# Decoding 64-bit weights in PSUM, taking their norms from Gram products, and ordering a whole kernel anew

## The chip, the core and the metric

The kernel runs on one core of a Trainium2 chip. The core has five engines with a queue each: TensorE (PE in the profile, its weight loads PEld) multiplies and writes PSUM, VectorE (DVE), ScalarE (ACT) and GpSimd (POOL) compute, SyncE (SP) issues all DMAs of this kernel. The metric is the device time of one execution in microseconds, the median of several runs; the profile is one further execution with its own time.

## What is computed

Windowed attention with global tokens, followed by a two-layer network on its output. Batch 8, 8 heads of 64, 512 local and 32 global tokens each. The two weight matrices arrive as 64-bit floats, everything else as 32-bit.

```python
s_g = scale * q_g @ k_all.T ;  out_g = softmax(s_g) @ v_all        # k_all: global, then local
s_ll = where(abs(i - j) <= 32, scale * q_l @ k_l.T, -1e9)
s_l = concat([scale * q_l @ k_g.T, s_ll]) ;  out_l = softmax(s_l) @ [v_g, v_l]
x = concat([out_g, out_l])            # 8 x 544 rows of 512
h = x @ w_in                          # 512 x 2048
g = where(h >= 1, h, where(h <= -1, 0, (h + 1)**2 / 4))
return (g @ w_out).astype(float32)    # 2048 x 512
```

## The kernel before

**Precision.** All large products run in float16 pairs: a number x is scaled by a power of two and split into a high half (a cast) and a low half (x minus the high half); a product of two such numbers is three float16 products. So every operand needs a scale, found from a norm, then a cast and a subtraction. Transposes go by DMA or by TensorE with an identity (`turn`, L622).

**Weights.** Each matrix is 16 tiles of 128 x 512 64-bit numbers (`w_in` by `load_win` L637 straight into its place, `w_out` by `load_wout` L687 into tiles called `twin` in the trace). `decode` (L539) makes a 32-bit float of the two 32-bit words of each number. A first instruction takes the magnitude of the high word times 2^-111 into `m`, a tile of the SBUF room (ScalarE, or GpSimd where the string `mags` has "p"); a second takes the three top bits of the low word (VectorE, or two GpSimd instructions where `shifts` has "p"); a third, on VectorE, shifts `m` left by three and joins the bits. `signed` (L568), again on VectorE, joins the sign and writes the tile. `win_decode` (L641) and `wout_decode` (L693) then multiply the upper 16 bits of the magnitudes by a matrix of ones, 4 products of 128 columns for a tile of w_in, one of 512 for a tile of w_out, summed over tiles, so that every partition holds the column sums. `w_scale` (L571) takes their maximum, once for tiles 0 to 7 and 8 to 15 of w_in, three times for w_out. `halves` (L594) splits a tile by one of the ways in `CODES` (L1449), three letters for who scales, casts and subtracts; "e" scales and subtracts in PSUM with one float32 product (two records in the trace) and one of float16, and "s" keeps the magnitude in place without `signed` and multiplies by sign and scale later.

**Attention and network.** For each batch and each block of 128 rows `att_a` (L897) makes scores of two heads, exponentials, a cast and a subtraction for the probabilities' halves, and a transpose; `att_b` multiplies by v; `att_x` divides and splits. `moe1` (L1114) makes one group of four w_in tiles for 128 rows in 48 products, `act` (L1099) the activation and its halves, `moe2` the product with w_out. The first three of 16 blocks of 256 rows go that way; later ones use a Winograd form of the same product with 7 instead of 8 block products.

**Order.** The program is recorded as named steps, cut into segments of one engine each (`segments`, L172), and put in order by a list scheduler (`schedule`, L226). It takes the segment with the earliest due time on each engine, from costs (`cost`, L130) and `deadlines` (L331), counts free places in three shared stores (`ROOMS`: 48 SBUF tiles of 2 KB, 6 of 4 KB and 8 PSUM banks; `CAPS` limits each kind), and `LATER` (L1451) shifts each step's due time by a given number of microseconds. Strings in `T` (L1563) choose an engine for each small operation: `subs`, `casts`, `adds` for the probabilities of batches 0 and 1, `glow` for the low half of an activation, `lows` for that of an attention output, `splits`, `turns`, `halves`, `mags`, `shifts`. All engines execute their queue in that order. All instructions pass through one helper, so the profile puts nearly all of them on L1440; loads are on L1442.

Of the kernel before, what the change touches and what calls it, by code (L numbers as in the profile page):

```python
# [128 lines left out]

def cost(engine, op, a, k, outs, ins, tiles):  # L130
# [8 lines left out]
    if engine == "sync":  # L139
        b = o.shape[0] * n * mybir.dt.size(o.dtype)  # L140
        if op == "dma_start_transpose":
            return 1300.0, b / 186.0
        run = min(tuple(x.ap[-1])[1] * mybir.dt.size(x.dtype) for x in (o, ins[0]))
        return 560.0, b / (215.0 if run < 512 else 340.0)
    if engine == "scalar":
        ptr = any(free(x) == 1 for x in ins[1:])
        if "accum_out" in k:
            own = 190 if ptr else 95
        elif mybir.dt.size(o.dtype) == 2:
            own = 185 if ptr else 90  # L150
# [207 lines left out]
def attention_moe(nc, memory, q_l, k_l, v_l, q_g, k_g, v_g, w_in, w_out, out):  # L358
# [3 lines left out]
    P = 128  # L362
# [60 lines left out]
    ps_h = bank("ps_h")  # L423
    ps_o = bank("ps_o")
# [114 lines left out]
    def decode(words, mag, who, whom):  # L539

        raw = words.rearrange("p (c t) -> p c t", t=2)
        lo, hi = raw[:, :, 0], raw[:, :, 1]
        m = tmp.tile([P, DM], F32, tag="tmp", name="wmag")

        if whom == "p":
            nc.gpsimd.tensor_scalar(m, hi.bitcast(F32), 2.0 ** -111, 1.0, op0=ALU.mult, op1=ALU.mult)  # L550
# [14 lines left out]
    def upper(mag):  # L565
        return mag.bitcast(BF16).rearrange("p (c t) -> p c t", t=2)[:, :, 1]
# [20 lines left out]
    def scaled_id(n, s, whos):  # L587
        if not any(x[0] == "e" for x in whos):
            return None
# [4 lines left out]
    def halves(w, a, s, sid, who):  # L594
# [3 lines left out]
        if who[0] == "e":  # L598
            o = ps_h.tile([P, DM], F32, tag="p", name="wps")
# [22 lines left out]
    def turn(who, o, i):  # L622
# [5 lines left out]
        t = ps_h.tile([P, 8, P], F16, tag="p", name="turn")  # L628
# [12 lines left out]
    def win_decode(f):  # L641
        words = w32[f].bitcast(I32)
        raw = words.rearrange("p (c t) -> p c t", t=2)
        if halves_of([f])[0][0] == "s":

            decode(words, raw[:, :, 0].bitcast(F32), T["shifts"][f], T["mags"][f])
            mag = w32[f].bitcast(BF16).rearrange("p (c t) -> p c t", t=4)[:, :, 1]
        else:
            m = decode(words, None, T["shifts"][f], T["mags"][f])
            mag = upper(m)  # L650
            signed(raw[:, :, 1], raw[:, :, 1], m)
# [41 lines left out]
    def wout_decode(f):  # L693
        raw = W.pop(("rawo", f))
        m = decode(raw.rearrange("p c t -> p (c t)"), None, T["shifts"][NF + f], T["mags"][NF + f])
        mag = upper(m)
        signed(wo32[f], raw[:, :, 1], m)
        n, gs = next((n, gs) for n, gs in enumerate(WOUT) if f // WG in gs)
        f0, f1 = gs[0] * WG, (gs[-1] + 1) * WG
        if f == f0:  # L700
            W["no"] = ps_o.tile([P, DM], F32, tag="p", name=f"won{f}")
        nc.tensor.matmul(W["no"], ones, mag, start=(f == f0), stop=(f == f1 - 1))
# [3 lines left out]
        nc.vector.tensor_reduce(mx, W["no"], axis=AX.X, op=ALU.max)  # L706
# [156 lines left out]
    def moe_scales(key, d, tv, first, c0=0, c1=4):  # L863
# [8 lines left out]
        nc.vector.tensor_scalar(bd, (wt if first else W["tma"])[:, c0:c1], tv[:, 0:1], 2.0 ** 28, op0=ALU.mult, op1=ALU.mult)  # L872
# [537 lines left out]
    for name, (t, _, fn, a) in sorted(steps.items(), key=lambda x: x[1][:2]):  # L1410
# [8 lines left out]
            ps_h=4, ps_o=3, ps_s=2, ps_x=1)  # L1419
# [5 lines left out]
def build(tc, *args):  # L1425
# [4 lines left out]
    with ExitStack() as ctx:  # L1430
# [5 lines left out]
        with tc.manual_schedule():  # L1436
# [14 lines left out]
LATER = {"Lk00": -99.8, "Lk01": 23.8, "Lk02": 37.7, "Lk10": 212.4, "Lk11": -53.4, "Lk12": 178.5, "Lk20": 42.4, "Lk21": 24.7,  # L1451
# [146 lines left out]
```

## Time and profile before

| what | us |
|---|---|
| median of 3 runs | 946.48 |
| lowest and highest run | 943.96, 948.40 |
| the profiled execution | 945.8 |
| its span, first to last instruction | 944.0 |
| PE busy in the span | 861.5 |
| VectorE, ScalarE, GpSimd busy | 786.0, 642.9, 434.0 |

A busy share is an average over stages: PE is nearly idle while the first weights and keys arrive, and nearly full from 240 us on. Busy times of PE are those of its pipelined products, so what counts is when it idles. A wait names the last thing that the waiting instruction lacked, an engine with the tile that it wrote ("DVE room": a tile of the SBUF room), or a DMA.

### The profile page before, as it was taken

Reading aid. Unit: us, or ns where it says so; the run is one execution under the profiler, and the core shown is the slowest. Engines: PE = TensorE matmul, PEld = TensorE weight load, DVE = VectorE, ACT = ScalarE, POOL = GpSimd, SP = SyncE. Lnnn points to the kernel's source line nnn. Section 1 sums busy time; section 2 is a strip of 40 time slices with the busy share of each in tenths; the row PEclk is TensorE's granted clock in tenths of the full one; section 3 lists DMA queues with packets and bytes.
Section 4 is the critical chain, followed back from the end, with each engine's and each line's share of the span. In section 5 each row is a group of like instructions: output and inputs, shape, how many; then the busy total and the mean of one; then the engine's idle time right before and its main releaser. Section 6 shows DMA issues by size and latency. Waiting matters only on the chain.

```text
span 944.0 us, 30674 instructions
## 1 busy us (share of the span) xinstructions
PE 861.5 (91%) x12204; PEld 642.3 (68%) x12207; DVE 786.0 (83%) x2079; ACT 642.9 (68%) x1545; POOL 434.0 (46%) x450
## 2 busy tenths in 40 slices
PE   0466889998989998999999999999999999999998
PEld 0343757567858686667677767867686777786864
DVE  2989899889777997789989979999999897878642
ACT  3799979567767784768676757777776765565441
POOL 9154576624233634363364333554446245536231
PEclk9979999999999999999999999999999999999999
DMA  9999748958977899849995847989997777353101
GB/s 267 265 201 236 166 105 152 174 128 119 161 172 151 136 188 169 169 83 159 193 180 94 158 98 138 173 137 170 155 166 138 152 112 141 57 105 66 35 2 45
DMA packets 407823, 134.91 MB, mean 143 GB/s; under 512 B 384128, under 2 KB 393344, under 8 KB 407680
## 3 DMA queue, kind: packets, MB, share of 16 engines
q1 hardware_dynamic: 407680, 132.96, 74.6%
q8 instruction: 95, 1.56, 0.7%
q14 instruction: 48, 0.39, 0.1%
HBM read 43.52 MB, written 8.91 MB: 56 GB/s over the span
## 4 chain that ended last, share of the span: by engine, by line
PE 63%; DVE 9%; DMA 7%; ACT 3%; issue 2%; SPq 2%; POOL 1%; DVEq 0%; ACTq 0%; POOLq 0%
PE bank L1440 63%; DVE room L1440 5%; DMA room<-const_pb 3%; ACT room L1440 2%; DMA room<-room 2%; DVE bank L1440 1%; DMA room<-in_k_g_dram 1%; DMA room<-in_k_l_dram 1%; SPq L1440 1%; DMA room<-in_q_l_dram 1%; ACT junk_junk L1440 1%; DVE const_pb L1440 1%; SPq L1442 1%; POOL const_pb L1440 1%; POOL room L1440 1%
## 5 line engine op out<-in xcount | busy, mean ns | idle before, releaser
L1440 PEld LDWEIGHTS <-room 128*128 128x128 f16 (+2 forms) x5136 | 288.2, 98 | 223.5 <-issue 25.0
L1440 PE MATMUL bank<-weights_w,room 128*128 128x512 f16 x1632 | 373.1, 380 | 3.6 <-ACT room L1440 2.1
L1440 POOL TENSOR_TENSOR room<-room,room 128x512 f16<-128x512 f32 (+5 forms) x200 | 223.7, 1125 | 212.3 <-ACT room L1440 185.0
L1440 PE MATMUL bank<-room,weights_w 128*128 128x128 f16 (+1 forms) x4032 | 235.2, 216 | 6.7 <-DVE room L1440 4.0
L1440 PEld LDWEIGHTS <-weights_w 128*128 128x128 f16 x4032 | 221.1, 98 | 18.3 <-issue 5.3
L1440 POOL TENSOR_TENSOR const_pb<-room,const_pb 128x384 f16<-128x384 f32 (+1 forms) x117 | 124.2, 1063 | 225.5 <-DVE const_pb L1440 81.4
L1440 ACT CAST room<-room 128x512 f16<-128x512 f32 (+3 forms) x212 | 122.0, 583 | 81.3 <-DVE room L1440 65.3
L1440 ACT ACTIVATE room<-room,small_nb 128x192 f32<-128x192 f32 (+1 forms) x256 | 117.2, 459 | 55.2 <-DVE small_nb L1440 45.0
L1440 PE MATMUL bank<-room,room 96*128 96x64 f16 (+3 forms) x2816 | 128.3, 196 | 9.4 <-DMA room<-const_pb 6.1
L1440 PE MATMUL bank<-room,twin 128*128 128x128 f16 (+1 forms) x2160 | 123.1, 216 | 3.3 <-DMA room<-room 2.4
L1440 PEld LDWEIGHTS <-twin 128*128 128x128 f16 x2160 | 115.5, 98 | 6.3 <-DMA room<-room 2.5
L1440 DVE CUSTOM_DVE_ANT_0 room<-bank,const_mask,batch_small_q 128x192 f32<-128x192 f32 (+1 forms) x256 | 99.0, 426 | 11.2 <-PE bank L1440 10.4
L1440 ACT ACTIVATE junk_junk<-room 128x512 f16<-128x512 f32 (+1 forms) x120 | 75.2, 626 | 46.0 <-DMA room<-in_k_l_dram 16.7
L1440 ACT ACTIVATE room<-bank,batch_small_ms 128x512 f32<-128x512 f32 (+1 forms) x114 | 84.4, 750 | 28.8 <-DVE bank L1440 18.3
L1440 DVE SCALAR_TENSOR_TENSOR bank<-bank,batch_small_ms,room 128x512 f32<-128x512 f32 (+1 forms) x114 | 82.1, 724 | 16.6 <-ACT room L1440 16.5
L1440 DVE SCALAR_TENSOR_TENSOR room<-room,batch_small_ms,bank 128x512 f32<-128x512 f32 (+1 forms) x114 | 80.7, 711 | 0.8
L1440 ACT COPY room<-bank 128x512 f32<-128x512 f32 (+2 forms) x98 | 56.5, 587 | 22.3 <-PE bank L1440 20.9
L1440 DVE CAST const_pb<-room 128x384 f16<-128x384 f32 (+1 forms) x109 | 51.4, 474 | 19.9 <-DMA room<-const_pb 13.2
L1440 DVE TENSOR_TENSOR bank<-bank,room 128x512 f32<-128x512 f32 (+1 forms) x60 | 39.0, 656 | 27.0 <-PE bank L1440 26.9
L1440 DVE SCALAR_TENSOR_TENSOR room<-room,batch_small_ms,room 128x512 f32<-128x512 f32 (+1 forms) x60 | 54.1, 901 | 0.8 <-ACT room L1440 0.2
L1440 DVE TENSOR_TENSOR room<-room,room 128x512 f16<-128x512 f32 (+1 forms) x55 | 40.9, 751 | 12.7 <-ACT room L1440 12.6
L1440 ACT ACTIVATION_READ_ACCUMULATOR room<-room,small_nb 128x1 f32 x256 | 48.1, 188 | 0.0
(153 smaller groups left out, 959.1 us busy)
## 6 DMA issues: line engine op xcount, KB each, us to landing
room<-room SPq DMA_DIRECT2D x80, 128.0 KB, 3.2
weights_w<-in_moe_w_in_dram SPq DMA_DIRECT2D x32, 256.0 KB, 4.2
room<-in_q_l_dram SPq DMA_DIRECT2D x32, 256.0 KB, 4.2
twin<-in_moe_w_out_dram SPq DMA_DIRECT2D x32, 256.0 KB, 3.9
out_dram<-room SPq DMA_DIRECT2D x32, 256.0 KB, 2.7
room<-in_k_l_dram SPq DMA_DIRECT2D x24, 256.0 KB, 4.3
room<-in_v_l_dram SPq DMA_DIRECT2D x24, 256.0 KB, 3.9
room<-const_pb SPq DMA_TRANSPOSE x124, 3.4
```

The costliest lines, as they stand in the source:

```text
L1440: getattr(getattr(tc.nc, engine), op)(*a, **k)
L1442: r = tc.nc.sync.dma_start(*a)
```

## The change

The magnitudes that come from ScalarE, and all results of the third instruction that are not kept in place, lie in a PSUM bank (`ps_m`) instead of the SBUF room, so `signed` reads one operand from PSUM. [...] The float32 way of `halves` and the transposes on TensorE get bank kinds of their own. The costs of the planner change, and the order and the strings were searched anew; no DMA is added or removed but for one transpose.

```diff
 def cost(engine, op, a, k, outs, ins, tiles):
-        run = min(tuple(x.ap[-1])[1] * mybir.dt.size(x.dtype) for x in (o, ins[0]))
+        run = min(stretch(x) for x in (o, ins[0]))
         return 560.0, b / (215.0 if run < 512 else 340.0)
...
-            own = 185 if ptr else 90
+            own = 185 if ptr else 45 if ins[0].tensor.name in tiles and tiles[ins[0].tensor.name][2] else 90
...
+    if engine == "gpsimd" and o.dtype == I32:
+        return 125 + n * 3.6, 0
     if engine == "gpsimd":
         return (125 + n * (1.93 if len([x for x in ins if free(x) > 1]) > 1 else 1.05) if op != "memset" else 60 + n * 0.82), 0
...
-    if n > 16 and o.dtype == I32 and len(big) == 1:
-        return 525, 0
     if len(big) > 1 or ps or op == "tensor_reduce":
-        return (80 if op == "tensor_tensor" else 135) + m / 0.96 + (40 if "accum_out" in k else 0), 0
+        return 70 + 60 * len([x for x in ins if free(x) == 1]) + m / 0.96 + (8 if "accum_out" in k else 0), 0
...
     def decode(words, mag, who, whom):
-        m = tmp.tile([P, DM], F32, tag="tmp", name="wmag")
+        up = words.bitcast(U16).rearrange("p (c t) -> p c t", t=4)[:, :, 1]
+        m = ps_m.tile([P, DM], F32, tag="p", name="mag") if whom == "a" or mag is None else None
+        got = m
         if whom == "p":
-            nc.gpsimd.tensor_scalar(m, hi.bitcast(F32), 2.0 ** -111, 1.0, op0=ALU.mult, op1=ALU.mult)
+            got = tmp.tile([P, DM], F32, tag="tmp", name="wmag")
+            nc.gpsimd.tensor_scalar(got, hi.bitcast(F32), 2.0 ** -111, 1.0, op0=ALU.mult, op1=ALU.mult)
         else:
-            nc.scalar.activation(m, hi.bitcast(F32), AF.Abs, scale=2.0 ** -111)
+            nc.scalar.activation(got, hi.bitcast(F32), AF.Abs, scale=2.0 ** -111)
-        if who == "p":
+        if who == "a":
+            nc.scalar.activation(lo, up, AF.Copy, scale=2.0 ** -13, bias=2.0 ** -14 - 0.5)
+        elif who == "p":
...
-        nc.vector.scalar_tensor_tensor(mag.bitcast(I32), m.bitcast(I32), 3, lo, op0=ALU.logical_shift_left, op1=ALU.bitwise_or)
+        nc.vector.scalar_tensor_tensor(mag.bitcast(I32), got.bitcast(I32), 3, lo, op0=ALU.logical_shift_left, op1=ALU.bitwise_or)
...
-    def w_scale(norms, tag, n, pl, room=1.0):
+    def w_scale(squares, tag, n, pl, room=1.0):
         e, t2, t8, s = cols(pl, tag, tag, n, n, n, n)
+        root(e, squares)
+        norms = t2
+        all_max(norms, e, tag)
         nc.vector.tensor_scalar(e.bitcast(I32), norms.bitcast(I32), 0x7F000000, None, op0=ALU.bitwise_and)
-        inverse(t2, s, e, 2.0 ** -51, 2.0 ** -13 * room)
+        inverse(t2, s, e, 2.0 ** -51, 2.0 ** -10 * room)
...
     def win_decode(f):
         for k in range(NK):
-            nc.tensor.matmul(W["n"][:, f % WG], ones, mag[:, k * P:(k + 1) * P], start=(k == 0), stop=(k == NK - 1))
+            x = half[:, k * P:(k + 1) * P]
+            nc.tensor.matmul(W["n"][:, f % WG], x, x, start=(k == 0), stop=(k == NK - 1))
...
     def wout_decode(f):
-        nc.tensor.matmul(W["no"], ones, mag, start=(f == f0), stop=(f == f1 - 1))
+        for k in range(NK):
+            x = half[:, k * P:(k + 1) * P]
+            nc.tensor.matmul(W["no"][:, k], x, x, start=f == f0 and k == 0, stop=f == f1 - 1, skip_group_check=True)
...
-            ps_h=4, ps_o=3, ps_s=2, ps_x=1)
+            ps_m=3, ps_w=3, ps_t=3, ps_h=4, ps_o=3, ps_s=2, ps_x=1)
...
-T = dict(... adds="vvvvvv1vvvvvvvvvvvvvavvvvvvvvv1v",
-         subs="pppppppppppvvvpppppppvpvvpppppvp", glow="pppppppppppvpppv",
-         turns="aaaaaaaaaadddddddddddddddddddddddddddddddddddddddddddddddddd", casts="aaaaaaaaaaaaaaaavvavvvavvvvvvavv",
-         mags="aaapaaaaaaaaaaaaaaaaaaaaaaaaaaaa", lows="ppppvpvv", halves="aaaaaaaaabacacacdecchccbddfdcbef",
-         shifts="pppvpvvpvvvvvvvvvvvvvvvvvpvvvvvv", splits="vvvvvvvvvvvpvvvpvvvpvppp", ...
+T = dict(... adds="vvvvvv1vv11vvaa11vaa1vv1av1vv1v1",
+         subs="ppppppppppppppppvvpvvpvpvvppvpvv", glow="ppvppvpvvpvpppvv",
+         turns="aaaaaaaaaadddddddddddddddddddddddddddadddddddddddddddddddddd", casts="aaaaaaaaaavaavaavvavvavvvvavvaav",
+         mags="pappaaaaaaaaaaaaaaapaaaapaaaaaaa", lows="vppvvpvp", halves="aaaaaaaaaiacacacdeccdcedcifdcdef",
+         shifts="vppapvvpvpvvvvvvvvvvvvvvapavvvvv", splits="vvvvvvvvvvvpvvppvvvpppvp", ...
```
`stretch` is new and gives the longest contiguous run of bytes of an access pattern. Nearly all entries of `LATER` differ; those of the new list are fewer and mostly smaller.

More of the change, by code (lines that the diff above doesn't have):

```diff
@@ L127, in free, with stretch @@
     return n
+def stretch(ap):
+    n = 1
+    for st, c in reversed([tuple(d) for d in ap.ap][1:]):
+        if st != n and c > 1:
+            break
+        n *= c
+    return n * mybir.dt.size(ap.dtype)
 def cost(engine, op, a, k, outs, ins, tiles):
@@ L423, in attention_moe @@
     ps_h = bank("ps_h")
+    ps_m = bank("ps_m")
+    ps_w = bank("ps_w")
+    ps_t = bank("ps_t")
     ps_o = bank("ps_o")
@@ L587, in scaled_id @@
     def scaled_id(n, s, whos):
-        if not any(x[0] == "e" for x in whos):
-            return None
         t = cp.tile([P, P], F32, tag="sid", name=f"sid{n}")
@@ L598, in halves @@
         if who[0] == "e":
-            o = ps_h.tile([P, DM], F32, tag="p", name="wps")
+            o = ps_w.tile([P, DM], F32, tag="p", name="wps")
             nc.tensor.matmul(o, sid, a, start=True, stop=False)
@@ L627, in turn @@
         n = i.shape[0]
-        t = ps_h.tile([P, 8, P], F16, tag="p", name="turn")
+        t = ps_t.tile([P, 8, P], F16, tag="p", name="turn")
         for c in range(8):
@@ L643, in win_decode @@
         raw = words.rearrange("p (c t) -> p c t", t=2)
+        half = w32[f].bitcast(BF16).rearrange("p (c t) -> p c t", t=4)
         if halves_of([f])[0][0] == "s":
             decode(words, raw[:, :, 0].bitcast(F32), T["shifts"][f], T["mags"][f])
-            mag = w32[f].bitcast(BF16).rearrange("p (c t) -> p c t", t=4)[:, :, 1]
+            half = half[:, :, 1]
         else:
-            m = decode(words, None, T["shifts"][f], T["mags"][f])
-            mag = upper(m)
-            signed(raw[:, :, 1], raw[:, :, 1], m)
+            signed(raw[:, :, 1], raw[:, :, 1], decode(words, None, T["shifts"][f], T["mags"][f]))
+            half = half[:, :, 3]
         if f % WG == 0:
@@ L694, in wout_decode @@
         raw = W.pop(("rawo", f))
-        m = decode(raw.rearrange("p c t -> p (c t)"), None, T["shifts"][NF + f], T["mags"][NF + f])
-        mag = upper(m)
-        signed(wo32[f], raw[:, :, 1], m)
+        signed(wo32[f], raw[:, :, 1], decode(raw.rearrange("p c t -> p (c t)"), None, T["shifts"][NF + f], T["mags"][NF + f]))
+        half = wo32[f].bitcast(BF16).rearrange("p (c t) -> p c t", t=2)[:, :, 1]
         n, gs = next((n, gs) for n, gs in enumerate(WOUT) if f // WG in gs)
@@ L700, in wout_decode @@
         if f == f0:
-            W["no"] = ps_o.tile([P, DM], F32, tag="p", name=f"won{f}")
-        nc.tensor.matmul(W["no"], ones, mag, start=(f == f0), stop=(f == f1 - 1))
+            W["no"] = ps_o.tile([P, NK, P], F32, tag="p", name=f"won{f}")
+        for k in range(NK):
+            x = half[:, k * P:(k + 1) * P]
+            nc.tensor.matmul(W["no"][:, k], x, x, start=f == f0 and k == 0, stop=f == f1 - 1, skip_group_check=True)
         if f < f1 - 1:
@@ L705, in wout_decode @@
         mx = sm.tile([P, 1], F32, tag="womx", name=f"womx{f}")
-        nc.vector.tensor_reduce(mx, W["no"], axis=AX.X, op=ALU.max)
+        nc.vector.tensor_reduce(mx, W["no"], axis=AX.XY, op=ALU.max)
         t8, so = w_scale(mx, f"wo{n}", 1, cp)
@@ L870, in moe_scales @@
         bd, rb, s2, sg, hs, a1, a2 = [t[:, c0:c1] for t in d["ms"][:7]]
-        nc.vector.tensor_scalar(bd, (wt if first else W["tma"])[:, c0:c1], tv[:, 0:1], 2.0 ** 28, op0=ALU.mult, op1=ALU.mult)
+        nc.vector.tensor_scalar(bd, (wt if first else W["tma"])[:, c0:c1], tv[:, 0:1], 2.0 ** 26, op0=ALU.mult, op1=ALU.mult)
         nc.vector.tensor_scalar(bd, bd, 1.0, 2.0 ** 60, op0=ALU.max, op1=ALU.min)
@@ L1449 @@
 CODES = {"a": "eaa", "b": "sap", "c": "pap", "d": "aap", "e": "aav", "f": "pav", "g": "sav", "h": "eav", "i": "vap", "j": "eva"}
-LATER = {"Lk00": -99.8, "Lk01": 23.8, "Lk02": 37.7, "Lk10": 212.4, "Lk11": -53.4, "Lk12": 178.5, "Lk20": 42.4, "Lk21": 24.7,
[111 rows of a table removed]
-T = dict(late=1, fast=3, cb=200, cbs=5, lk0=4.19, lq0=1.76, lv0=30, sk=12, sq=14, adds="vvvvvv1vvvvvvvvvvvvvavvvvvvvvv1v",
-         subs="pppppppppppvvvpppppppvpvvpppppvp", glow="pppppppppppvpppv",
-         turns="aaaaaaaaaadddddddddddddddddddddddddddddddddddddddddddddddddd", casts="aaaaaaaaaaaaaaaavvavvvavvvvvvavv",
-         mags="aaapaaaaaaaaaaaaaaaaaaaaaaaaaaaa", lows="ppppvpvv", halves="aaaaaaaaabacacacdecchccbddfdcbef",
-         shifts="pppvpvvpvvvvvvvvvvvvvvvvvpvvvvvv", splits="vvvvvvvvvvvpvvvpvvvpvppp", att=1.35, s0=60, s1=100, s2=254.09,
-         wd0=4, wds=2.06, wd8=19.2, wdt=1.9, wh=1.5, whs=1.4, od=58.2, ods=2.2, oh=0.7, ohs=0.92, e0=25.78, e1=70, e2=120.0,
-         e3=156.0, w0=24.7, w1=24.34, w2=25.15, w3=25.51, z1=18.29, lq1=24, lv2=24.36, sv=34, sqb=35.02, pk2=20.4, pk3=30,
+LATER = {"Lk00": 2.5, "Lk01": -54.4, "Lk02": -50, "Lk10": 49.4, "Lk11": 1.2, "Lk12": 173.6, "Lk20": 64.2, "Lk21": 200.3,
[105 rows of a table added]
+T = dict(late=1, fast=3, cb=200, cbs=5, lk0=4.19, lq0=1.76, lv0=30, sk=12, sq=14, adds="vvvvvv1vv11vvaa11vaa1vv1av1vv1v1",
+         subs="ppppppppppppppppvvpvvpvpvvppvpvv", glow="ppvppvpvvpvpppvv",
+         turns="aaaaaaaaaadddddddddddddddddddddddddddadddddddddddddddddddddd", casts="aaaaaaaaaavaavaavvavvavvvvavvaav",
+         mags="pappaaaaaaaaaaaaaaapaaaapaaaaaaa", lows="vppvvpvp", halves="aaaaaaaaaiacacacdeccdcedcifdcdef",
+         shifts="vppapvvpvpvvvvvvvvvvvvvvapavvvvv", splits="vvvvvvvvvvvpvvppvvvpppvp", att=1.35, s0=60, s1=100, s2=254.09,
+         wd0=4, wds=2.06, wd8=19.2, wdt=1.9, wh=1.5, whs=1.4, od=58.2, ods=2.2, oh=0.7, ohs=0.92, e0=25.78, e1=70, e2=120,
+         e3=156, w0=24.7, w1=24.34, w2=25.15, w3=25.51, z1=18.29, lq1=24, lv2=24.36, sv=34, sqb=35.02, pk2=20.4, pk3=30,
          pk4=45.8, pq2=28.03, pq4=44, pv=35.24, pvs=0.33, lw=0.54, lo=32.46, los=2.12)
```

3 lines of the change are left out of this document (removed), and 216 rows, old and new, of the table LATER.

## The prediction

> **What bounds the kernel now.** I read the page first, then busy time by stretches, then who waits for whom before the first MoE product, then the groups of instructions with their shapes.
>
> ```profile
> span 944.0 us, 30674 instructions
> PE 861.5 (91%) x12204; PEld 642.3 (68%) x12207; DVE 786.0 (83%) x2079; ACT 642.9 (68%) x1545; POOL 434.0 (46%) x450
> ```
> ```profile
> core 0: us, PE busy (x) PEld busy (x) DVE busy (x) ACT busy (x) POOL busy (x), PEclk, DMA share, GB/s
> 0.00:24.00 24.00, 1.38 (x11) 1.15 (x12) 5.82 (x9) 7.14 (x13) 21.27 (x39) 1.00 0.92 266
> 24.00:94.00 70.00, 40.29 (x399) 26.98 (x400) 63.93 (x184) 62.42 (x138) 27.11 (x25) 0.93 1.01 233
> 94.00:240.00 146.00, 132.51 (x1962) 102.20 (x1960) 133.44 (x374) 113.04 (x280) 78.51 (x76) 1.00 0.73 140
> 240.00:400.00 160.00, 149.64 (x2118) 113.72 (x2116) 131.22 (x358) 110.17 (x277) 65.02 (x68) 1.00 0.91 165
> 400.00:900.00 500.00, 497.38 (x7277) 375.19 (x7274) 436.66 (x1131) 339.04 (x815) 234.18 (x233) 1.00 0.73 128
> 900.00:944.00 44.00, 40.29 (x460) 23.06 (x456) 14.92 (x29) 11.14 (x25) 7.85 (x11) 1.00 0.08 25
> ```
> Subtract PE's busy time from each stretch: PE is idle 22.6, 29.7, 13.5, 10.4, 2.6 and 3.7 us. From 400 us on TensorE is the bound and nothing but less TensorE work helps. The 66 us of idle PE before 240 us are what can be won, and there VectorE is nearly full: 63.9 of 70 us, then 133.4 of 146. In the first 24 us everybody waits for the loads (DMA share 0.92), which the change leaves as they are.
>
> ```profile
> PE bank L1440 <- DVE room L1440: 33.7, 10, 12.0
> ...
> DVE room L1440 <- DMA weights_w<-in_moe_w_in_dram: 12.8, 2, 10.2
> PE bank L1440 <- ACT weights_w L1440: 11.7, 8, 2.9
> ...
> DVE room L1440 <- POOL weights_w L1440: 4.5, 2, 2.6
> ```
> ```profile
> 94.19 2.84 PE L1440 MATMUL bank<-room,weights_w 128*128 128x128 f16 x48
> ```
> The first fence has waits before 94 us, the second the first group of MoE products. PE waits 33.7 us for VectorE and 11.7 us for ScalarE's first halves of the weights; VectorE waits 4.5 us for GpSimd's shifts. So a microsecond less on the chain loads, decode, scale, attention, first product is worth up to a microsecond of the end; one in the steady part is worth nothing.
>
> **The change, part by part.**
>
> *Magnitudes in PSUM.* Each of 32 weight tiles has two VectorE passes over 128x512 words, and both read two SBUF tiles now.
>
> ```profile
> L1440 DVE SCALAR_TENSOR_TENSOR weights_w<-weights_w,room 128x512 int32<-128x512 int32 x15 | 11.5, 777 | 0.1
> L1440 DVE SCALAR_TENSOR_TENSOR room<-room,weights_w 128x512 int32<-128x512 int32 x15 | 10.7, 717 | 17.4 <-DMA weights_w<-in_moe_w_in_dram 12.8 <-POOL weights_w L1440 4.5
> L1440 DVE SCALAR_TENSOR_TENSOR weights_w<-twin,room 128x512 int32<-128x512 int32 x7 | 6.6, 950 | 0.0
> L1440 DVE SCALAR_TENSOR_TENSOR room<-room,twin 128x512 int32<-128x512 int32 x7 | 5.4, 774 | 0.0
> ```
> ```profile
> L1440 DVE SCALAR_TENSOR_TENSOR weights_w<-twin,room x10: 676/682/1047, 94.0 to 155.6; 128x512 int32<-128x512 int32 x10
> L1440 DVE SCALAR_TENSOR_TENSOR room<-room,twin x9: 675/693/1631, 96.9 to 151.9; 128x512 int32<-128x512 int32 x9
> ```
> ```profile
> L1440 DVE SCALAR_TENSOR_TENSOR room<-room,twin 128x512 int32<-128x512 int32 x16 | 13.8, 869 | 3.2 <-ACT room L1440 1.9 <-POOL twin L1440 1.2
> L1440 DVE SCALAR_TENSOR_TENSOR weights_w<-twin,room 128x512 int32<-128x512 int32 x16 | 13.7, 854 | 0.0
> ```
> The first fence is before 94 us, the second gives min/median/max after it, the third the whole run. The median is some 685 ns and single ones take up to 1631: they stood behind something, and GpSimd's SBUF work ran beside them. With one operand in PSUM I expect the plain 685. Before 94 us that is 15 x 92 + 15 x 32 + 7 x 265 + 7 x 89 ns = 4.4 us; in the whole run 15 x 92 + 15 x 32 + 16 x 184 + 16 x 169 ns = 7.5 us. If the cause is another, it is 0.
>
> ```profile
> L1440 DVE TENSOR_TENSOR bank<-bank,room 128x512 f32<-128x512 f32 x52 | 35.6, 692 | 18.0 <-PE bank L1440 17.8 <-ACT room L1440 0.2
> L1440 DVE TENSOR_TENSOR room<-bank,small_rc 128x512 f32<-128x512 f32 x32 | 21.8, 681 | 0.8 <-PE bank L1440 0.8
> L1440 ACT ACTIVATE room<-twin 128x512 f32<-128x512 f32 x16 | 10.6, 670 | 0.0
> ```
> No row has an int32 pass on PSUM; the nearest two-operand passes on a bank take 681 and 692 ns, so I add nothing for PSUM itself (bounds: -5 to +10 ns each). [...] ScalarE's magnitude pass (670 ns into SBUF) I leave at its price; one that writes PSUM from SBUF is not in the trace, and bank-sourced copies are no slower than SBUF ones, so within 0.1 us each.
>
> *Norms by Gram products.*
> ```profile
> L1440 PE MATMUL bank<-room,const_ones 128*128 128x128 bf16 x60 | 7.3, 277 | 31.3 <-DVE room L1440 31.3
> L1440 PE MATMUL bank<-weights_w,const_sid 128*128 128x512 f32 x26 | 16.0, 698 | 0.0
> L1440 PE MATMUL bank<-weights_w,const_negid 128*128 128x512 f16 x13 | 5.1, 395 | 10.9 <-ACT weights_w L1440 10.9
> L1440 PE MATMUL bank<-room,const_ones 128*128 128x512 bf16 x13 | 5.0, 388 | 3.9 <-DVE room L1440 3.9
> ```
> w_in keeps 64 products of 128 columns; each loads its own stationary tile now, beside the product before. w_out gets 64 of 7.3/60 = 0.12 us for 16 of 0.38: +1.6 us. One tile fewer takes the float32 way through PSUM (13 to 12): (16.0 + 5.1)/13 = -1.6 us. TensorE comes out even.
>
> ```profile
> L1440 DVE TENSOR_SCALAR small_dg<-const_negid,small_amv 128x128 bf16<-128x128 f16 x8 | 2.7, 341 | 0.0
> L1440 DVE TENSOR_REDUCE small_amv<-bank 128x1 f32<-128x128 f32 x8 | 2.2, 278 | 0.4 <-PE bank L1440 0.4
> L1440 DVE TENSOR_SCALAR small_nb<-small_nb 128x2 f32<-128x2 f32 x125 | 29.6, 241 | 0.2
> ```
> Each of five scales gains a root and a maximum over the partitions: 341 + 278 + two small operations of at most 241 = 1.1 us of VectorE with one product between. Two lie before 94 us (2.2 us, on the chain to the halves), three behind (3.3 us). The norm products now read the signed words, one VectorE pass later; the next tile's passes are queued there anyway, so nothing is charged.
>
> *Codes: who does what.* The strings give ScalarE three shifts and one query turn (whose eight transposes go to TensorE, beside its idle time), and GpSimd four magnitudes for nine subtractions less; both have room after 24 us. VectorE matters:
>
> ```profile
> L1440 DVE TENSOR_TENSOR room<-room,room 128x512 f16<-128x512 f32 x42 | 31.9, 768 | 11.5 <-ACT room L1440 11.4
> L1440 DVE TENSOR_TENSOR const_pb<-room,const_pb 128x448 f16<-128x448 f32 x4 | 2.5, 621 | 0.0
> L1440 DVE TENSOR_SCALAR weights_w<-weights_w 128x512 int32<-128x512 int32 x11 | 4.9, 465 | 0.0
> L1440 POOL TENSOR_TENSOR room<-room,room 128x512 f16<-128x512 f32 x137 | 173.7, 1275 | 176.5 <-ACT room L1440 155.8 <-PE bank L1440 12.0 <-DMA room<-const_pb 3.7
> ```
> Before 94 us: one shift less, a second pass for the tile that loses its code "s": about 0, so with the scales +2.0 and the relief -4.4 the chain gains 2.4 us. After it: five MoE low halves and one attention output 6 x 768, three more subtractions of probabilities 3 x 621, the scales 3.3, eight more small additions 8 x 241, one weight tile's scaling 0.5 (another tile's low half comes, a cast goes), less two shifts and a split (1.7): 4.6 + 1.9 + 3.3 + 1.9 + 0.5 - 1.7 = 10.5 us, less 3.1 us of relief: +7.4 us of VectorE work where it idles 12.6 us. GpSimd needs 1275 ns for what VectorE does in 768, so those results come earlier. Between 0 and +7.4, I take +1.5, near the end that fits the idle time.
>
> *Costs and order.* The loads' order on SP's queue, the transposes' and every engine's order change, and no DMA is added. What the old order did not know is visible:
> ```profile
> L1440 POOL TENSOR_SCALAR weights_w<-weights_w 128x512 int32<-128x512 f32 x5 | 10.5, 2098 | 0.4
> L1440 POOL TENSOR_SCALAR weights_w<-weights_w 128x512 f32<-128x512 uint16 x5 | 5.9, 1183 | 6.1 <-DMA weights_w<-in_moe_w_in_dram 5.8
> ```
> A GpSimd shift takes 2.1 + 1.2 = 3.3 us; `cost` (L130) gave both instructions 663 ns, 1.3 us together, and now gives 663 and 1968. Five of the six belong to w_in, whose tiles all products wait for. VectorE's waits for them (4.5 us here, 1.2 us for a w_out tile) are such plan errors. PE's 11.7 us behind ScalarE come from the same queues. An order made from true prices can win from 0 to 5.7 + 11.7 = 17.4 us; I take the 5.7 and a third of the 11.7 (a row of eight waits, each under 2.9, not all removable): -9.6.
>
> **Sum** against the profiled execution (945.8 us: span 944.0 and 1.8 around it): -2.4 + 1.5 - 9.6 = -10.5, so 935.3; the median of the runs, 946.48, lies 0.7 above, so 936.0.
>
> **Rivals.**
> *No change* (943 to 950). The relief is eaten by the work moved to VectorE, and the new order is as far from the chip as the old one: -2.4 + 1.5 = -0.9, 945.6. For it: VectorE's work grows by 5 us in all, and an order made from better estimates is still one of estimates. Against: the waits above are visible and priced.
>
> *Slower: banks.* Now ScalarE's decode needs one of the eight PSUM banks that the products use.
> ```profile
> 78.75 0.65 ACT L1440 ACTIVATE room<-twin 128x512 f32<-128x512 f32 x1
> ```
> ```profile
> 81.67 0.64 DVE L1440 SCALAR_TENSOR_TENSOR weights_w<-twin,room 128x512 int32<-128x512 int32 x1
> ```
> A magnitude lives from 78.75 to 82.31, 3.6 us; the tile view above has nine or ten w_out decodes behind 94 us, beside the first products. With three magnitudes, four products' banks and one output bank all eight are gone, and the next score or product waits; on ScalarE's queue exponentials and relus stand behind a magnitude that waits. From about that filling on, nine decodes that each hold one group of 48 (2.84 us) back by half cost 12.8 us: 946.5 - 0.9 + 12.8 = 958. Against: the planner counts banks and can place w_out's decodes where scores do not need them.
>
> *More* (921). All 17.4 us of order, and half of the 10.4 us idle at 240 to 400: 946.5 - 2.4 - 17.4 - 5.2 = 921.5. For it: those later waits are order too; against: loads at full DMA share before 94 us set a floor.
>
> **How the numbers follow.** Forecast case 0.48 (926.7 to 941.6: order between -17.4 and -4, the moved work 0 or 1.5), more 0.14 (912 to 926), no change 0.20, banks 0.18 (951 to 965). A measurement of this kernel tells about 0.5% (4.7 us) from no change; faster by more is 0.48 + 0.14 = 0.62, within 0.20, slower 0.18. The range 918 to 955 leaves out half of the case of more and somewhat over half of the bank case, under 0.2 in all. The predicted time is the likeliest case's, 936.
>
> **What would show it.** Relief: the int32 passes with a bank at 680 to 700 ns mean, whatever GpSimd does. Order: the first group of 48 products before 94 us, PE's wait for ScalarE's weights well under 11.7 us, PE idle before 240 us some 55 us for 66. Scales: five more products with ones, 1 to 2 us each between the last norm and the first half. Wrong: bank tiles as releasers of ScalarE's magnitudes or of PE (the bank rival); int32 passes still at 800; the first product no earlier than 94 us; PE busy from 400 us on below 497 of 500.

## The result: 1.1 % slower, and the profile after

| | before | changed |
|---|---|---|
| median of 4 runs, us | 947.25 (943.96 to 948.40) | 957.76 (954.79 to 959.21) |
| profiled execution, its span | 945.8, 944.0 | 958.5, 956.8 |
| mean granted TensorE clock in it | 0.993 | 0.982 |

The ratio is 1.0113, with a 95% interval of 1.0076 to 1.0149. Forecast were 936 us and a range of 918 to 955.

The head of the page after, then busy time by stretches (columns: busy us and instructions of each engine, PE's clock, DMA share, GB/s):

```profile
span 956.8 us, 30761 instructions
PE 876.8 (92%) x12265; PEld 651.5 (68%) x12265; DVE 783.5 (82%) x2113; ACT 641.0 (67%) x1549; POOL 421.0 (44%) x445
```
```profile
0.00:24.00 24.00, 2.40 (x17) 1.67 (x17) 7.88 (x19) 10.07 (x23) 18.65 (x40) 1.00 0.99 259
24.00:94.00 70.00, 48.11 (x382) 30.47 (x383) 61.88 (x197) 59.55 (x130) 24.98 (x25) 0.85 1.00 232
94.00:240.00 146.00, 131.16 (x1980) 102.06 (x1978) 135.16 (x375) 111.05 (x278) 66.31 (x68) 1.00 0.71 140
240.00:400.00 160.00, 153.74 (x2148) 115.91 (x2146) 134.93 (x375) 115.47 (x290) 68.61 (x70) 0.97 0.95 164
400.00:900.00 500.00, 488.41 (x7027) 365.68 (x7024) 411.44 (x1090) 322.50 (x789) 225.86 (x222) 1.00 0.75 129
```

The row that changed sides is the steady part. From 400 to 900 us PE was idle for 2.6 us before and is idle for 11.6 us now. Followed along the same products in both traces (roughly, since their order differs), the changed kernel is some 2 us behind at 400 us, 4 at 600, 9.5 at 730 and 12.7 at 850. The loss arises where no weight is decoded any more. What PE waits for there (engine and tile waited for: us in total, times, longest):

```profile
PE bank L1449 <- DMA room<-const_pb: 6.1, 7, 1.5
PE bank L1449 <- DMA room<-room: 2.0, 2, 1.2
PE bank L1449 <- DVE room L1449: 1.2, 1, 1.2
PE bank L1449 <- DVE small_nb L1449: 0.9, 2, 0.7
PE bank L1449 <- ACT room L1449: 0.9, 2, 0.5
```

`room<-const_pb` is the transposing DMA that turns the probabilities for the product with v. Before, there was one such wait of 2.1 us. The chain of work that ended last can be followed back only to 707 us in the changed kernel. From there to 860 us, by share, in the kernel before and then in the changed one:

```profile
by line: PE bank L1440 100.1%
```
```profile
by line: PE bank L1449 44.2%; DMA room<-const_pb 10.7%; DVE room L1449 9.6%; issue 6.1%; SPq L1449 3.6%; DMA room<-in_v_l_dram 3.5%; DMA room<-in_q_l_dram 3.4%; POOL room L1449 3.0%; POOL const_pb L1449 2.8%; DMA room<-room 2.2%; DVE bank L
```

TensorE was the whole chain there and is less than half of it now. The rest is many small pieces, DMAs and SyncE's queue (SPq) among them. That queue, in the changed kernel's timeline (start, us until the last of the row is issued, count):

```profile
249.99 0.53 SPq L1451 DMA_DIRECT2D room<-in_q_l_dram  x1
250.57 0.57 SPq L1451 DMA_DIRECT2D room<-in_v_l_dram  x1
...
260.16 4.01 SPq L1449 DMA_TRANSPOSE room<-room  x3
264.27 0.53 SPq L1451 DMA_DIRECT2D room<-in_k_l_dram  x1
264.89 3.21 SPq L1449 DMA_TRANSPOSE room<-room  x2
268.20 2.00 SPq L1449 DMA_DIRECT2D room<-room  x3
...
273.92 1.83 SPq L1449 DMA_DIRECT2D room<-room  x3
275.86 1.75 SPq L1451 DMA_DIRECT2D room<-in_v_l_dram  x3
...
284.99 3.47 SPq L1449 DMA_TRANSPOSE room<-const_pb  x2
288.56 0.53 SPq L1451 DMA_DIRECT2D room<-in_q_l_dram  x1
289.19 1.18 SPq L1449 DMA_DIRECT2D qg_qgb<-qg_qga  x2
```

Between the first and the last of these rows the queue has hardly a gap: 41 issues, 13 of them transposes, take 40.4 us. The planner (`cost`, sync branch) prices a transpose at 1300 ns and another DMA at 560, which is 13 x 1.30 + 28 x 0.56 = 32.6 us. Part of the excess can be waiting: the profile puts 10.8 us of SyncE's waits for other engines into these 40.4 us, within the issues' own durations. Neither price was touched by the change; the order was sought anew under them.

PE waits 3.2 us, from 286.5 us on, for the first of the two transposes of `const_pb` at 284.99, near the end of that row. The last write into a tile of that name before it was GpSimd's:

```profile
280.10 0.92 POOL L1449 TENSOR_TENSOR const_pb<-room,const_pb 128x384 f16<-128x384 f32 x1 [0.29 <-DVE const_pb L1449]
```

It ended at 281.02 us, so that transpose was issued at least 4.0 us after its input was there, behind another transpose and three plain DMAs. Of PE's seven waits for such transposes from 400 us on, five follow one that was issued 0.7 to 4.3 us after the last such write, longer than PE then waited; in the other two (1.1 and 0.6 us) it was 0.1 and 0.4 us, and the queue does not explain them.

The planner's own end, by its own prices, is 933.5 us for the kernel before and 918.6 for the changed one: it promised 15 us that the chip did not give.

### The profile page after: what moved, and what is told of

The parts are those of the page before. It is cut to its first block, busy times and chain, and to the rows that moved or that the text cites. A ratio compares the mean times of both kernels' runs of the same rounds, so it can differ in the third digit from the quotient of the medians.

```text
span 956.8 us, 30761 instructions
## 1 busy us (share of the span) xinstructions
PE 876.8 (92%) x12265; PEld 651.5 (68%) x12265; DVE 783.5 (82%) x2113; ACT 641.0 (67%) x1549; POOL 421.0 (44%) x445
## 5 line engine op out<-in xcount | busy, mean ns | idle before, releaser
L1449 PEld LDWEIGHTS <-room 128*128 128x128 f16 (+1 forms) x5144 | 291.6, 99 | 229.9 <-issue 22.6
L1449 POOL TENSOR_TENSOR room<-room,room 128x512 f16<-128x512 f32 (+3 forms) x194 | 215.7, 1118 | 236.0 <-ACT room L1449 192.0
L1449 PEld LDWEIGHTS <-weights_w 128*128 128x128 f16 (+1 forms) x4160 | 232.1, 99 | 43.1 <-DVE weights_w L1449 24.9
L1449 POOL TENSOR_TENSOR const_pb<-room,const_pb 128x448 f16<-128x448 f32 (+1 forms) x114 | 122.5, 1075 | 191.6 <-DVE const_pb L1449 92.5
L1449 ACT CAST room<-room 128x512 f16<-128x512 f32 (+2 forms) x213 | 122.1, 582 | 87.2 <-DVE room L1449 60.8
L1449 ACT ACTIVATE room<-room,small_nb 128x224 f32<-128x224 f32 (+1 forms) x256 | 117.2, 459 | 56.6 <-DVE small_nb L1449 45.4
L1449 PE MATMUL bank<-room,room 96*128 96x64 f16 (+3 forms) x2816 | 131.6, 197 | 24.4 <-DMA room<-const_pb 13.0
L1449 DVE CUSTOM_DVE_ANT_0 room<-bank,const_mask,batch_small_q 128x224 f32<-128x224 f32 (+1 forms) x256 | 98.5, 425 | 6.1 <-PE bank L1449 3.4
L1449 DVE CAST const_pb<-room 128x448 f16<-128x448 f32 (+1 forms) x109 | 51.2, 470 | 24.9 <-DMA room<-const_pb 20.4
L1449 DVE TENSOR_TENSOR room<-room,room 128x512 f16<-128x512 f32 (+1 forms) x62 | 47.7, 774 | 12.7 <-ACT room L1449 12.5
```

Source lines behind the costliest of these rows:

```text
L1449: getattr(getattr(tc.nc, engine), op)(*a, **k)
```

## The experiments

Three theories went in. A: the new order has no room for what SyncE's queue really takes. B: the new decode costs the time. C, the prediction's own premise: from 400 us on TensorE is full whatever the order. Later ones are named in the expectations. To hold an order, each segment's due time is set to its start in the plan to be copied, and "every engine held to it" means that an engine may only take the next one:

```diff
 def plan(steps, tiles, prio, names, hop, slack, landing, ahead):
     segs = segments(steps, tiles, prio, names)
...
+    seen = {}
+    for g in segs:
+        i = seen[g.step] = seen.get(g.step, -1) + 1
+        g.prio = HELD[g.step][i]
     order, taken, _ = schedule(segs, tiles, hop, slack, landing, ahead)
...
-                    if g.ready > now:
+                    if g.ready > now or g.n != turns[e][-1]:
                         continue
```

The kernel before had a median of 946.8 to 947.8 us beside the experiments, and all ratios are to it; the changed kernel was not run again beside them.

| run | what | us | ratio, 95% interval | planner's own end |
|---|---|---|---|---|
| e1 | changed, late order as before | 944.65 | 0.9970 (0.9946 to 0.9994) | 921.2 |
| e2 | new decode, old codes, old order from 170 us | 957.85 | 1.0123 (1.0098 to 1.0149) | 934.6 |
| e3 | before, 40 issues more | 958.67 | 1.0130 (1.0097 to 1.0163) | 940.5 |
| e4 | changed, no searched shifts | 961.08 | 1.0143 (1.0115 to 1.0171) | 935.6 |
| e5 | changed, order sought with new DMA prices | 944.52 | 0.9976 (0.9958 to 0.9994) | 917.6 |
| e6 | old decode, likewise | 934.72 | 0.9887 (0.9853 to 0.9922) | 922.5 |
| e7 | changed, 30 issues fewer | 947.93 | 1.0006 (0.9990 to 1.0021) | 919.5 |
| e8 | new decode, old codes, in e6's order | 944.58 | 0.9973 (0.9957 to 0.9989) | 923.7 |
| e9 | as e5, from another start | 944.53 | 0.9969 (0.9954 to 0.9984) | 918.6 |
| e10 | as e6, other random moves | 941.70 | 0.9954 (0.9934 to 0.9974) | 920.0 |
| e11 | e8 without the longer scale chain | 939.91 | 0.9940 (0.9920 to 0.9960) | 921.5 |
| e12 | e8 with magnitudes in SBUF | 952.16 | 1.0064 (1.0045 to 1.0083) | 928.2 |

**e1, only the late order undone.**

> The changed program; up to about 430 us every engine keeps the changed kernel's order, from there on each of the five runs its segments in the order of the kernel before. Nothing is left out. Theory A (SyncE's queue): the new order puts transposing DMAs behind others in SyncE's queue just before their products are due, and from 400 us on the chain passes through that queue. With the old late order the PE waits after 430 us (about 9 us in the changed kernel) go, and the time falls by 8 to 12 us to 946-950. Theory B (the decode: banks, Gram products, ScalarE's magnitudes): the loss comes with the decode, which is untouched: 955-960. Theory C (the prediction's: from 400 us on TensorE is full whatever the order, so the loss lies before): 955-960 too, with PE's idle time after 430 us unchanged.

Measured 944.65 us, 13.1 less than the changed kernel: theory A, a little more than it expected, while B and C expected nothing. PE after 430 us, in the changed kernel and in e1 (rows of busy time, then e1's only wait):

```profile
430.00:900.00 470.00, 458.41 (x6637) 343.71 (x6636) 383.54 (x1023) 302.16 (x746) 208.65 (x206) 1.00 0.76 131
```
```profile
430.00:900.00 470.00, 466.39 (x6859) 352.64 (x6857) 403.96 (x1061) 316.77 (x766) 212.84 (x215) 1.00 0.73 131
```
```profile
PE bank L1455 <- DMA room<-const_pb: 3.6, 2, 2.4
```

The same instructions in another order give 8 us of PE back; the waits fall from 11.1 us to 3.6. The chain from 707 to 860 us is TensorE's again:

```profile
by line: PE bank L1455 100.0%
```

So the late order is the loss, and everything else of the change together is worth 944.65 - 947.84 = -3.2 us. (e1's profiled execution, at 949.78 us, is the slowest of its ten.)

**e3 and e7, the suspected cost added and taken away.** e3 cuts the swap of a query tile's halves in four. e7 replaces it by one copy and so leaves the swap out: the scores of those batches come from unswapped halves.

```diff
 def swap_q(b, c):
-        dma(u[0:D], t[D:2 * D])
-        dma(u[D:2 * D], t[0:D])
+        for h0, h1 in [(0, H // 2), (H // 2, H)] if b >= 4 else [(0, H)]:
+            dma(u[0:D, h0:h1], t[D:2 * D, h0:h1])
+            dma(u[D:2 * D, h0:h1], t[0:D, h0:h1])
```
```diff
 def swap_q(b, c):
+        if b >= 2:
+            dma(u, t)
+        else:
             dma(u[0:D], t[D:2 * D])
             dma(u[D:2 * D], t[0:D])
```

> The kernel before in its own order, every engine held to it, but in batches 4 to 7 each of the two DMAs that swap a query tile's halves is cut in two by heads: 40 more issues on SyncE, the same bytes. Theory A: an issue takes about 0.64 us of SyncE's in-order queue (three in a row 1.83 to 2.00 us in the changed kernel's trace), so 26 us of queue are added between some 390 and 820 us, where the transposes stand behind them; where SyncE is already late they end on TensorE: slower by 8 to 18 us, 955-965, with PE waits for const_pb transposes that the kernel before does not have. Theory C: TensorE is full there and SyncE waits for others half of the time, so at most 2 us: 946-949.

> The changed kernel in its own order, every engine held to it, but in batches 2 to 7 one DMA copies a query tile whole in place of two that swap its halves: 30 issues fewer on SyncE, the same bytes; the scores of those batches are left computed from unswapped halves. Theory A: 30 x 0.64 = 19 us of SyncE's queue are taken out between some 200 and 820 us, of which the part that lies ahead of late transposes comes back: faster than the changed kernel by 4 to 11 us, 947-954, with fewer PE waits for const_pb transposes. Theory B and C: as the changed kernel, 956-959.

Both as A expected. 40 issues more cost the kernel before 958.67 - 947.84 = 10.8 us, 30 fewer give the changed one 957.76 - 947.93 = 9.8 us, with the same bytes and every engine's order held. That is 0.27 and 0.33 us of the end for an issue of some 0.64 us. The planner saw the first in part (940.5 for 933.5) and the second not at all (919.5 for 918.6): in the changed kernel's order the queue costs the chip what the plan does not know. PE's waits from 400 to 900 us, the largest row of e3 and then of e7 (whose profiled execution, at 943.32 us, is the fastest of its ten):

```profile
PE bank L1448 <- DMA room<-const_pb: 8.4, 4, 3.5
```
```profile
PE bank L1458 <- DMA room<-const_pb: 2.9, 2, 1.7
```

In the kernel before PE was idle for only 2.6 us there and SyncE's issues filled some 307 of the 500 us, and still two fifths of each added issue reached the end. So the queue can be late in a burst (in the timeline above the transpose of 284.99 us was issued at least 4.0 us after its input was there, behind another transpose and three plain DMAs) while it is far from full on average. Theory C falls.

**e4, the search taken away.**

> The changed program with LATER empty: the planner's deadlines alone under the new prices, no searched shifts. The planner's own end is 935.6 us for it and 918.6 us for the changed kernel, so it holds the search to be worth 17.0 us. Theory A: what the search won it won partly in time that SyncE does not have, so on the chip it is worth well under 17 us: 957 plus 3 to 12, so 960-969. Theory B and C: prices right enough, the search is worth what it says: about 974.

Measured 961.08, in A's range. By the planner the searched shifts are worth 17.0 us; on the chip 961.08 - 957.76 = 3.3, which the two intervals do not tell from nothing.

**e5 and e6, the order sought with new DMA prices.** Both issue prices go up, and `LANDING`, the planner's time from the end of a transfer to its use, goes down:

```diff
         if op == "dma_start_transpose":
-            return 1300.0, b / 186.0
+            return 1500.0, b / 186.0
-        return 560.0, b / (215.0 if run < 512 else 340.0)
+        return 680.0, b / (215.0 if run < 512 else 340.0)
...
-HOP, SLACK, LANDING, AHEAD = 290.0, 600.0, 1500.0, 5
+HOP, SLACK, LANDING, AHEAD = 290.0, 600.0, 900.0, 5
```

With these three numbers and the old orders held, the planner's end moves to 944.3 us for the kernel before (its span was 944.0) and to 946.8 for the changed one: the 15 us between them are gone, though on the chip the second span is 12.8 us longer, not 2.5. The two issue prices do it: with them alone the planner ends at 958.8 and 958.0, and `LANDING` sets the level. e5 searches the changed program's order anew under them, e6 that of the kernel before.

> The changed program, nothing left out, with three numbers of its planner set to what the traces show and the order sought anew under them: a transposing DMA 1500 ns on SyncE's queue for 1300 (two in a row 2.67 to 3.47 us in the changed kernel's trace), another DMA 680 ns for 560, and 900 ns for 1500 from the end of a transfer to its use. The planner's own end is 917.6 us, while for the changed kernel's order, held, these numbers give 946.8, and for that of the kernel before 944.3. Theory A (SyncE's queue): the chip now follows the plan but for the clock, which cost the earlier kernels 0 to 12 us: 922-938, PE busy above 494 of the 500 us from 400 us on, and the chain there through TensorE. Theory B (the decode costs what was lost): no order mends it, 950-960. Theory C (the order in the steady part is worth nothing): what can be won lies before 240 us, 945-957.

> The kernel before with its own decode (magnitudes in SBUF, norms by products with ones, its codes) and the changed kernel's prices with the same three numbers set as in e5, the order sought anew for as long. The planner's own end is 922.5 us, 4.9 above e5's. Theory A: both decodes are faster than the kernel before by 10 to 25 us, and this one is 0 to 8 us behind e5: 924-942. Theory B: with the old decode the loss is gone and e5 has it, so this one is faster than e5 by about 10 us.

Both beat what they started from, by 957.76 - 944.52 = 13.2 and 946.83 - 934.72 = 12.1 us, the direction that A gave, and the late stage stays full; the row from 400 us on, e5 and then e6:

```profile
400.00:900.00 500.00, 494.81 (x7196) 371.17 (x7193) 427.16 (x1099) 329.49 (x801) 229.09 (x229) 1.00 0.73 128
```
```profile
400.00:900.00 500.00, 498.33 (x7300) 374.44 (x7298) 428.04 (x1116) 335.16 (x811) 232.61 (x234) 1.00 0.73 127
```

But e5 missed A's range (922 to 938), and e6 is 9.8 us ahead of it where A allowed at most 8 behind. That gap is what B had expected. So A explains the late loss, and something of B may be true as well. A's range for e5 rests on 0 to 12 us for the clock and on 900 ns from the end of a transfer to its use, which no run shows: the profiled executions have a mean clock of 0.984 in e5 and 0.992 in e6, without the time that this is worth, and from issue to landing a transpose of the probabilities takes 3.5 us in the changed kernel's trace (median). No run separates the issue prices from `LANDING`, nor either from the new search as such.

**e2 and e8, the new decode alone.**

> The new decode (magnitudes in PSUM, norms by Gram products) with the codes and the prices of the kernel before, and its order: from 170 us on as before, up to there as near to it as the new segments allow. Theory A: the decode itself is worth about nothing, so within 4 us of the kernel before: 944-951. Theory B: the decode carries the loss, 955-960. Both: VectorE's int32 passes with a bank at 675-700 ns.

> The changed program's decode (magnitudes in PSUM, Gram products, the longer scale chain) with the codes of the kernel before, in e6's order: from 250 us on as near to it as the planner's list allows, up to there sought anew under the same prices. The planner's own end is 923.7 us, 1.2 above e6's. e5 and e6 differ in the decode, in the codes and in the order at once. Theory B2 (the decode itself costs what parts e5 from e6, by the scale chain that is 6 us longer each time and delays the second group's halves): 941-948, with its curve behind e6's from the first 100 us on. Theory D (the codes cost it, by what they move to ScalarE and VectorE): 931-938, as e6. Theory E (neither: a plan made 5 us tighter comes that much later to the chip): 931-939 too, and e9 tells D from E.

The new decode takes its norms from the finished signed tile, not from the magnitudes in a bank (none of the 12204 products recorded before and the 12265 after reads a bank): each 128-column piece times itself, summed, puts sums of squares on the diagonal, so a scale needs a root and a maximum over the partitions.

e2 came out at 957.85: A missed it and B had it. It is no clean test, since its order up to 170 us was sought under the old prices of SyncE, and most of its loss against the kernel before (11 of 15 us, along the same products) arises between 205 and 250 us, when the last weight is long split (167 us). e8 repeats it under the new prices: 944.58, theory B2's range. It falls behind e6 early: the first group of 48 MoE products starts at 97.88 us, e6's at 93.51. The scale of w_in's second half shows one reason. VectorE's first and last operation on it, e6, then e8 (duration min/median/max, first and last start):

```profile
L1454 DVE TENSOR_SCALAR small_w<-small_wmx x1: 154/154/154, 55.7 to 55.7; 128x1 int32<-128x1 int32 x1
L1454 DVE RECIPROCAL small_w<-small_w x1: 164/164/164, 56.1 to 56.1; 128x1 f32<-128x1 f32 x1
```
```profile
L1453 DVE TENSOR_SCALAR small_w<-small_wmx x1: 146/146/146, 58.5 to 58.5; 128x1 int32<-128x1 int32 x1
L1453 DVE TENSOR_SCALAR small_dg<-const_negid,small_w x1: 626/626/626, 59.5 to 59.5; 128x128 bf16<-128x128 f16 x1
L1453 DVE TENSOR_REDUCE small_w<-bank x1: 274/274/274, 61.3 to 61.3; 128x1 f32<-128x128 f32 x1
L1453 DVE RECIPROCAL small_w<-small_w x1: 159/159/159, 63.7 to 63.7; 128x1 f32<-128x1 f32 x1
```

From 0.4 us the chain grew to 5.2, with under 1.5 us of VectorE's work in it. The rest lies between its links, while VectorE, busy for 61.06 of the 70 us there, has other work in its queue.

**e9 and e10, was it the order found?**

> The changed program with e5's prices, the order sought from another start: e1's (the late part as in the kernel before). The planner's own end is 918.6 us, 1.0 above e5's. Theory B2 and D (decode or codes cost some 10 us that no price shows): 941-948, as e5. Theory E (the order found makes it): it may fall anywhere from 930 to 948; under 938 would leave no room for a cost of 10 us in decode and codes.

> e6 once more with another order: the kernel before with its own decode and codes, the same prices, the order sought with other random moves for as long. The planner's own end is 920.0 us, 2.5 below e6's. So far four orders with the new decode ended at 944.5 to 944.7 (e1, e5, e8, e9) and one with the old decode at 934.7. Theory B2 (the new decode costs some 10 us): 931-938. Theory E (e6's order was a lucky one): 940-947.

e9 is at 944.53 like e5 and e8, although the planner gave it 918.6. e10 is at 941.70, in the range of theory E, which calls e6's order a lucky one: 7 us worse than e6, although the planner preferred it by 2.5. So a found order is worth several microseconds either way that the planner does not see. Against 944.5 the old decode is ahead by 2.8 (e10) to 9.8 us (e6); the intervals of e10 overlap those of e8 and e9, so the smaller figure is not shown to differ from nothing.

**e11 and e12, which part of the decode.** e11 leaves out the root and the maximum over the partitions, so each partition keeps a scale of its own and the output is another; e12 puts the magnitudes back into SBUF:

```diff
 def w_scale(squares, tag, n, pl, room=1.0):
-        root(e, squares)
-        norms = t2
-        all_max(norms, e, tag)
+        norms = squares
```
```diff
-        m = ps_m.tile([P, DM], F32, tag="p", name="mag") if whom == "a" or mag is None else None
+        m = tmp.tile([P, DM], F32, tag="tmp", name="mag") if whom == "a" or mag is None else None
```

> e8 with the part of each weight scale left out that the change adds: the square root's two operations and the maximum over the partitions (a VectorE pass, a product with ones, a VectorE maximum); each partition takes its scale from its own maximum, so the output is another. Magnitudes in PSUM and Gram products stay. The order up to 250 us is sought anew; the planner's own end is 921.5 us, 2.2 below e8's. In e8 a scale of w_in takes 5.3 us from its first small operation to the reciprocal where e6's takes 0.6 us. Theory B2 by the scale chain: 934-939, the first group of MoE products at 93-95 us as in e6 (e8: 97.9). Theory F (banks and Gram products, not the chain): 941-946.

> e8 with the magnitudes in SBUF again (the tiles that the kernel before used), norms still by Gram products and with the long scale chain: the PSUM part of the change undone alone. The order up to 250 us is sought anew for as long as e8's; the planner's own end is 928.2 us, 4.5 above e8's, since four SBUF tiles for the magnitudes are fewer than the banks give. Theory B2 by the scale chain: no gain, 944-952. Theory F (banks): 934-941, faster than e8. The int32 passes: 680-950 ns, by what GpSimd does beside them.

Without the chain 939.91 us, 4.7 less than e8, and the first group of 48 starts at 94.56: the start is in the range of B2, the end 0.9 us above it and below that of F. Without PSUM 952.16 us, 7.6 more than e8 (the planner says 4.5): no sign that the banks cost anything, against theory F. But both have an order up to 250 us of their own, and e6 and e10 lie 7.0 us apart by their orders alone, so neither difference is shown to be the decode's.

## Why the prediction was wrong, by its own steps

**The order (-9.6) is the step that failed**, and with it the premise that a microsecond "in the steady part is worth nothing" because TensorE is full there. TensorE's 2.6 us of idle time left little to win there, but an order that takes the slack of another queue costs time: e1 puts the late order alone at +13.1 us, more than the whole loss of 10.5. The gain did not come either: with the late order undone the whole change is worth -3.2 us (e1) where -10.5 was forecast. The prediction looked for wrong prices in VectorE's and GpSimd's branches of `cost` and called the new ones true. It did not hold the unchanged ones against the trace: a row of 41 SyncE issues takes a quarter longer than they say (40.4 us for 32.6, some of it perhaps waiting), and the queue of the kernel before was there to be read. "No DMA is added" was right and beside the point; what counts is what the order puts ahead of which transpose.

**PE's waits before 94 us** were to shrink to an earlier first product. PE's wait for ScalarE's weights went from 11.7 to 8.0 us, but the first MoE products came no earlier:

```profile
94.93 3.29 PE L1449 MATMUL bank<-room,weights_w 128*128 128x128 f16 x56
```

PE's idle time before 240 us fell from 65.8 to 58.3 us, not far from the 55 that was named as a sign. But from 24 to 94 us PE was busy for 48.11 us with 382 products where it had been for 40.29 us with 399, at a mean clock of 0.85 for 0.93: less idle time was not more work done.

**The relief (-7.5 us in the run) was right in kind and near in size.** The int32 passes with a bank, after:

```profile
L1449 DVE SCALAR_TENSOR_TENSOR weights_w<-weights_w,bank 128x512 int32<-128x512 int32 x16 | 10.8, 680 | 0.1
L1449 DVE SCALAR_TENSOR_TENSOR weights_w<-twin,bank 128x512 int32<-128x512 int32 x16 | 10.7, 674 | 0.1
L1449 DVE SCALAR_TENSOR_TENSOR bank<-bank,twin 128x512 int32<-128x512 int32 x14 | 9.7, 691 | 0.4 <-ACT twin L1449 0.2
L1449 DVE SCALAR_TENSOR_TENSOR bank<-bank,weights_w 128x512 int32<-128x512 int32 x13 | 8.8, 690 | 3.3 <-POOL weights_w L1449 2.9 <-ACT bank L1449 0.4
L1449 DVE SCALAR_TENSOR_TENSOR bank<-room,twin 128x512 int32<-128x512 int32 x2 | 2.5, 1240 | 1.2 <-POOL room L1449 1.1
L1449 DVE SCALAR_TENSOR_TENSOR bank<-room,weights_w 128x512 int32<-128x512 int32 x3 | 2.1, 699 | 10.5 <-POOL small_amv L1449 10.2 <-ACT weights_w L1449 0.3
```

They take 674 to 699 ns as forecast (680 to 700), but for two of the five that read GpSimd's magnitudes from SBUF (1240). In all 44.6 us for 50.4 before (the rows of the prediction and one more of 0.7): -5.8. (The 4.4 us before 94 us add up to 4.3 from the prediction's own products.) PSUM isn't needed for that speed: in e6 the passes over w_in take 681 and 712 ns in SBUF, with another order beside them.

**The scales (+2.0 before 94 us) were the term mis-sized.** 1.1 us of VectorE each was about right as work; the two before 94 us stand as 2.2 and then as 2.0 in the prediction. As a chain, from the first small operation to the reciprocal, w_in's second scale takes 55.9 to 62.7 us in the changed kernel and took 59.0 to 59.5 before. e11, without it, is 4.7 us faster than e8, with an order of its own.

**The moved work (+1.5)** shows no price: with the new codes (e5, e9) and the old ones (e8) the new decode ends at 944.5 us, each with an order of its own.

**The rival "banks" named 958 us** and the time came out there by accident. No bank that a magnitude filled appears among what PE waited for, ScalarE's magnitudes (632 and 639 ns into a bank) waited for loads alone, and e12, which undoes the banks, is slower. The sign named under "wrong", PE below 497 of 500 us from 400 us on, did come true (488.41), and so did the first product no earlier; by e1 the first pointed to the order, not to the banks.

**What stays open:** how much the decode costs with the best order for each. The runs say 2.8 to 9.8 us, and 4.7 us for the scale chain in one order; none of it was separated from the order, which alone moved e6 to e10 by 7.0. The fastest version is e6, 1.1% under the kernel before: its own decode, and the order sought with the new DMA prices.

## What to carry to other kernels

A search against a planner can spend the slack that the chip needs where the planner's prices are short, so compare its price for each queue, the DMA issues too, with the trace before letting it search, and mistrust an end that the chip has not confirmed: here the plans missed by 12 to 39 us (e6: 934.72 for 922.5; the changed kernel: 957.76 for 918.6). "TensorE is full" says that nothing can be won there, not that nothing can be lost. Look at what lies between the links of an added chain (5.2 us for under 1.5 us of VectorE's work), not only at the sum of its work.

## What the runs showed of the hardware

**An issue has its price on SyncE's queue.** In the timeline above three transposing DMAs in a row take 4.01 us, two 3.21 and 3.47, and three others 1.75 to 2.00 us: 1.3 to 1.7 us and about 0.6 us each. They are worth counting like an engine's instructions: by e3 and e7 0.27 and 0.33 us of each plain one reached the end.

**A short wait can be followed by half the clock.** PE's wait between 283 and 296 us in the changed kernel, and then busy time by stretches around it (PE first, its clock third from the end):

```profile
PE bank L1449 <- DMA room<-const_pb: 3.2, 1, 3.2
```

```profile
281.70:285.10 3.40, 3.40 (x31) 2.04 (x29) 3.40 (x10) 2.08 (x4) 0.17 (x1) 1.00 0.74 142
285.10:288.50 3.40, 1.41 (x34) 1.30 (x31) 1.10 (x2) 1.94 (x6) 1.46 (x1) 1.00 1.07 109
288.50:291.90 3.40, 2.22 (x16) 1.22 (x17) 2.18 (x4) 0.62 (x1) 1.74 (x2) 0.51 0.86 194
291.90:295.30 3.40, 3.40 (x9) 1.21 (x8) 3.40 (x12) 0.95 (x3) 2.83 (x3) 0.50 0.90 176
295.30:298.70 3.40, 3.40 (x34) 1.89 (x33) 2.72 (x7) 2.25 (x9) 1.17 (x2) 0.99 0.97 209
```

PE worked 1.41 of 3.4 us, and then had half its clock for two such stretches, 6.83 us (288.54 to 295.37 us). So a wait of 3.2 us was followed by half the clock, and so were one of 2.0 us (354.1 us; 3.41 us of half the clock from 356.80 us on) and one of 1.4 us (549.7 us; 3.41 us from 551.36 us on). Length alone does not decide: in the kernel before a wait of 2.6 us at 117.7 us was not (clock 1.00 from 117 to 130 us), while one of 2.1 us at 465.0 us was (3.41 us from 467.09 us on). What does decide, these traces do not show. The mean clock of the profiled executions was 0.993 before and 0.992 in e6, and between 0.973 (e4) and 0.985 (e8) where the decode is the changed kernel's; but e3, with the old decode and more waits, has 0.984 as well, and e10, with the old decode, 0.988. How much of each time that is was not separated. Executions of one kernel lie apart by up to 1%: e1's ten between 940.42 and 949.78 us, e6's six between 933.53 and 942.58.
